# A delta-rule attention and a maxout network: the second group's triangular solve in blocks of 16, kept in SBUF

## The chip, the core and the metric

The kernel runs on one core of a Trainium2 chip. The metric is the device time of one execution in microseconds, as the median of several runs. PE is the matrix engine, DVE the vector engine, ACT the scalar engine, POOL the general-purpose engine; SP only issues transfers.

## The reference

Inputs are q, k, v of 4 batches, 8 heads, 768 steps and 48 dimensions, and a beta per step, all float32. The first layer is a recurrence over the steps; its output, heads side by side, is the input of a maxout network with three weight matrices and an output matrix.

```python
k_n = k / (np.linalg.norm(k, axis=-1, keepdims=True) + 1e-06)
state = np.zeros((B, H, D, D), dtype=np.float32)
for t in range(S):
    kt, vt, bt = (k_n[:, :, t], v[:, :, t], beta[:, :, t, None])
    y[:, :, t] = np.einsum('bhd,bhde->bhe', q[:, :, t], state)
    v_old = np.einsum('bhde,bhd->bhe', state, kt)
    state = state + bt[:, :, :, None] * np.einsum('bhd,bhe->bhde', kt, vt - v_old)
...
x = attn_out.transpose(0, 2, 1, 3).reshape(B * S, H * D)      # 3072 x 384
h = np.maximum(np.maximum(x @ w1, x @ w2), x @ w3)            # 3072 x 768
out = h @ w_out                                               # 3072 x 384
```

## The kernel before

The 768 steps are cut into 12 chunks of 64 steps. Within a chunk the recurrence is a triangular system per batch and head, whose matrix comes from the products of the chunk's keys; its inverse, times beta, is held as `ut`. Two chunks are a group (six groups, `m` = 0 to 5; chunk `c` belongs to group `c // 2`), and the network works on a group's 512 tokens at a time (`ffn(m)`).

**The solve.** `solve(m)` inverts for all chunks of a group the diagonal blocks at once, one block to a partition: 2 chunks x 2 halves x 32 pairs of batch and head are 128 partitions, each with a block of 32x32 (`BL` = 32, `HB` = 16). One step of it is a pair of DVE instructions: a product into `tmp` (L561) and a subtraction from the solution `y` (L565); row by row, 31 pairs. `FINE` says how many groups are solved in finer blocks: with `m < FINE` each block of 32 is cut into two of 16, both in one instruction, which takes 15 pairs. Before, this is only group 0. Group 1 has its solution in PSUM (`y_p`, L524, one of the three buffers of two banks that all transposes, Gram products and joins take in turn through `ps_two`), zeroed by ACT at L525 and copied out to SBUF in two parts (L567 on ACT, L569 on DVE). Its place in SBUF, `y_bl`, lies in `wo_sb`, which is not yet filled with weights. Groups 2 and later have it in SBUF.

`solve` is a generator: each `yield` ends a step, and the loop around it takes so many steps at a time (`some(solving, n)`; `S1` in the table `FIRST` is one step). After the last step the solution goes to DRAM (`y_d`, L586, two transfers) and comes back in another layout into `ut` (L598, four transfers for each chunk), all on SP's queue.

**The joins.** Four products put the blocks together. Where blocks of 16 were solved, `halves_t` (three DVE transposes, L645 and L647), `halves_z` (32 products, L685, and an ACT copy L688) and `halves_u` (32 products, L696, and four ACT multiplications L700 that write into `ut`) make blocks of 32 of them. Then `join_z` (L713), `turn_t1` (L630, L632) and `join_u` (L726) make blocks of 64. `new` (L771) applies `ut` to the values. `halves_z` multiplies whole rows of 64, so the quarter of `ut` that no transfer writes must be zero: `new` clears it after use (L781) where the buffer is used again for a group in fine blocks. There are two buffers of `ut`, for chunks of even and odd number.

**The order around it.** All is ordered by hand: each engine executes its instructions in the order in which the code issues them, and waits at each for what it needs. After a first part (group 0's keys, solve and chunk 0), the loop over `ffn(0)` interleaves the network of group 0 with the rest of the attention. Each of its 31 steps, `i`, begins with one group of products of the network (L1224: three products of 256 columns for `i` < 18, of 512 behind, and from `i` = 27 the output's, L1262; two PSUM buffers), whose result ACT copies (L1232, one in three) or DVE takes the maximum with (L1238). Then come, by tables keyed by `i`: `FIRST` (the links of chunk 1, named by a letter and a number: `e` halves_z, `f` halves_u, `z` join_z, `d` turn_t1, `j` join_u, `k` and `q` products with the state, `u` new, `s` the state's update L801, `y` and `x` the output and its transposes, `T` transposes of queries, followed by a load of later queries on SP; `S` steps of the solve; `M` a mask L399, `P` Gram products of queries), `EARLY_LINKS` (the same letters for chunks 2 and 3, and `t` and `g`, transposes L338 and Gram products L415 of the units of group 2), a conversion of a piece of weights (`conv`: three ACT instructions L247 to L249, one DVE L259, one POOL L263), further steps of the solve, and loads of keys, queries, values and weights. Group 2's solve begins at `i` = 20.

Of the kernel before, what the change touches and what calls it, by code (L numbers as in the profile page):

```python
# [18 lines left out]
BL = 32  # L19
HB = 16  # L20
# [3 lines left out]
def kernel(  # L24
# [31 lines left out]
    nc = tc.nc  # L56
# [9 lines left out]
    GROUPS = UNITS // 4  # L66
    TOK = 512
    NK, NQ, NU = 8, 3, 2
    FINE = 1

    const = ctx.enter_context(tc.tile_pool(name="const", bufs=1))
    work = ctx.enter_context(tc.tile_pool(name="work", bufs=2))
# [19 lines left out]
    def ps_two(name):  # L92
        return pairs.tile([128, 2, 512], FP32, name=name, tag="two", bufs=3)
# [103 lines left out]
    t1 = [const.tile([128, 2, H, BL], FP32, name=f"t1{i}") for i in range(NU)]  # L197
# [254 lines left out]
    def in_rows(t):  # L452
        return t.rearrange("p s r -> p (s r)")[:, 0 : BL * BL].rearrange(
            "p (j i) -> p j i", i=BL
        )


    def in_wo(i):
        n = BL * BL + BL
        return wo_sb.rearrange("p t d -> p (t d)")[:, n * i : n * (i + 1)].rearrange(  # L460
            "p (s r) -> p s r", s=2
        )
# [44 lines left out]
    def solve(m):  # L507


        x = in_rows(xs[m])  # L510
        if m == 1:
            y_bl = in_wo(1)
        else:
            y_bl = work.tile([128, 2, HB * BL + HB], FP32, name="y_bl", bufs=1)
        done = y = in_rows(y_bl)
        zero = kpad[0][:, 0:1, D : D + 1]
        if m in (0, 2):
            nc.gpsimd.memset(y_bl, 0.0)
        elif m > 2:
            nc.scalar.copy(y, zero.to_broadcast(y.shape))  # L520
        bl = small("bl", BL)
        norm(bl, diagonal(x), small("root_bl", BL), small("nt_bl", BL))
        if m == 1:
            y = ps_two("y_p").rearrange("p b (j i) -> p (b j) i", i=BL)  # L524
            nc.scalar.copy(y, zero.to_broadcast(y.shape))  # L525
        if m:
            norms_of(m, bl)
            nc.vector.reciprocal(bl, bl)
        else:
            bl_0.append(bl)  # L530
            bl = small("inv_bl", BL)
            nc.vector.reciprocal(bl, bl_0[0])
        nc.vector.tensor_tensor(out=bl, in0=bl, in1=bl, op=ALU.mult)
        nc.vector.tensor_tensor(out=bl, in0=bl, in1=beta_bl[:, m] if m else beta_0, op=ALU.mult)
        if m > 2:
            nc.scalar.copy(diagonal(y), bl)
        else:
            (nc.vector if m == 1 else nc.gpsimd).tensor_copy(diagonal(y), bl)
        if m < FINE:
            size, xv, yv = HB, in_blocks(xs[m]), in_blocks(y_bl)  # L540
            xb = xv[:, :, :, 0:HB]
            by = bl.rearrange("p (s i) -> p s i", i=HB)[:, :, None, :]
            by = by.to_broadcast([128, 2, HB, HB])
        else:
            size, xv, yv = BL, x[:, None], y[:, None]
            xb, by = x, bl[:, None, :].to_broadcast([128, BL, BL])
        nc.vector.tensor_tensor(out=xb, in0=xb, in1=by, op=ALU.mult)
        yield
        for j in range(size - 1):
            a, b = j + 1, size - 1 - j  # L550
            n = BL // size
            tmp = work.tile([128, 256], FP32, name="tmp", bufs=1)
            t_v = tmp[:, 0 : n * a * b].rearrange("p (s c i) -> p s c i", s=n, i=b)
            row, column, rest = (
                xv[:, :, j, None, j + 1 : size],
                yv[:, :, 0:a, j, None],
                yv[:, :, 0:a, j + 1 : size],
            )
            if n == 1:
                row, column, rest, t_v = (t[:, 0] for t in (row, column, rest, t_v))  # L560
            nc.vector.tensor_tensor(  # L561
                out=t_v, in0=row.to_broadcast(t_v.shape),
                in1=column.to_broadcast(t_v.shape), op=ALU.mult,
            )
            nc.vector.tensor_tensor(out=rest, in0=rest, in1=t_v, op=ALU.subtract)  # L565
            if m == 1 and j == BL - 8:
                nc.scalar.copy(done[:, :, 0:HB], y[:, :, 0:HB])  # L567
            elif m == 1 and j == BL - 2:
                nc.vector.tensor_copy(done[:, :, HB:BL], y[:, :, HB:BL])  # L569
            yield  # L570
        if m == 0:
            back = in_rows(xs[0])
            nc.vector.transpose(out=back, in_=y.rearrange("p c i -> p i c"))
            yield
            for i in range(4):
                if i % 2:
                    n = H * (i == 3)
                    if n:
                        placed(0, i, nc.vector.tensor_copy, slice(0, n))
                    placed(0, i, nc.scalar.copy, slice(n, 2 * H))  # L580
                else:
                    placed(0, i, nc.vector.tensor_copy)
            return
        y_d = dram.tile([2, 2, B, H, BL, BL], FP32, name="y_d")
        for cc in range(2):
            nc.sync.dma_start(  # L586
                out=y_d[cc].rearrange("f b h i j -> (f b h) i j"),
                in_=done[64 * cc : 64 * (cc + 1)],
            )
        yield  # L590
        for cc in range(2):
            for half in range(2):
                for bb in range(2):
                    r0 = C * bb + BL * half
                    (
                        (nc.sync, nc.gpsimd) if m == GROUPS - 1
                        else one_queue if m or cc else both_queues
                    )[bb].dma_start(  # L598
                        out=ut[cc][
                            r0 : r0 + BL, :, :, BL * half : BL * (half + 1)  # L600
                        ].rearrange("p g h i -> p (g h) i"),
                        in_=y_d[cc, half, 2 * bb : 2 * bb + 2].rearrange(
                            "b h c i -> c (b h) i"
                        ),
                    )
            yield
# [158 lines left out]
    def new(c):  # L765
        rhs = rhss.pop(c)
        u = us[c] = both("u", D, 2)
        for hs, p_v, copy in heads_of(c, "p_u", D):
# [7 lines left out]
            copy(u[:, :, span(hs)], p_v)  # L776
        if c + NU < 2 * FINE:
            for bb in range(2):
# [497 lines left out]
    def some(gen, n):  # L1276
        for _ in range(n):
            if next(gen, gen) is gen:
                break

    conv = weights()
    solving = solve(0)
# [71 lines left out]
    for _ in range(2):  # L1354
# [17 lines left out]
    solving = solve(1)  # L1372
# [26 lines left out]
        GROUPS - 2: {0: 2, 1: 3, 2: 3, 3: 3, 4: 3, 5: 3},  # L1399
    }  # L1400
    EARLY_LINKS = {
        9: "k0 q0", 10: "t0", 11: "t1", 12: "g0", 13: "t2", 14: "g1", 15: "t3",
        16: "g2", 17: "g3", 18: "d0 d1 z0 z1", 19: "j0", 20: "j1 u0", 21: "s0",
        23: "k1 y0 q1", 24: "u1 x0", 25: "s1", 26: "y1", 28: "x1",
    }


    FIRST = {
        0: "e1 s0 S1 S1", 1: "f1 k1 S1 S1 S1", 2: "z1 d1 M2 S1 S1",
        3: "j1 S1 q1 M3 S1 S1", 4: "u1 T4", 5: "y1", 6: "s1 T5", 7: "x1 T6",  # L1410
        8: "T7", 14: "P4", 15: "P5", 21: "P6", 22: "P7",
    }

# [38 lines left out]
    for i, _ in enumerate(ffn(0)):  # L1452
        if i < 7:
            fetch(nc.sync if i else nc.gpsimd)
        if i == 0:
            scale(1, nrm_0[:, 1])
        if i == 1:
            load_q(4)
            load_q(5)
        if i == 2:  # L1460
            load_q(6)
        for _ in range(FETCHED.get(i, 0)):
            fetch(nc.gpsimd)
        if i == 25:
            some(conv, 1)
        if i == 21:
            some(solving, 3)
        queries(FIRST.get(i, ""))
        links(1, EARLY_LINKS.get(i, ""))
        if i == 20:  # L1470
            solving = solve(2)
            some(solving, 1)
        if i in CONVERTED:
            some(conv, 1)
        if i == 0:
            fetch(nc.gpsimd)
        if 3 < i < 14:
            some(solving, (3, 2, 2, 2, 3, 3, 3, 3, 2, 2)[i - 4])
        if i in (8, 13):
            prep_values(i // 4)  # L1480
        if i in (4, 8):
            for n in range(2):
                load_k(8 + 2 * (i > 4) + n, (nc.gpsimd, nc.gpsimd))
        if i == 11:
            load_q(11, (nc.gpsimd, nc.gpsimd))
        if i in (3, 9, 10, 21):
            load_v((3, 9, 10, 21).index(i) + 2)
        if i == 18:
            blocks(2)
        if i == 23:  # L1490
            prep_values(4)
        if i > 21:
            some(solving, (3, 1, 2, 2, 3, 5, 5, 5, 5)[i - 22])
        if i in (27, 28, 29):
            load_blocks(i - 15, nc.sync)
        if i in (15, 17, 19, 22, 25, 27):
            less_first((15, 17, 19, 22, 25, 27).index(i))
        if 27 <= i < 30:
            turn_first((2 * (i - 27), 2 * (i - 27) + 1))
# [5 lines left out]
    for m in range(1, GROUPS):  # L1505
        for i, _ in enumerate(ffn(m)):
# [6 lines left out]
            if m + 2 < GROUPS:  # L1513
                if i == 6:
                    blocks(m + 2)
                if i == 8:
                    solving = solve(m + 2)
# [37 lines left out]
```

## Time and profile before

| | us |
|---|---|
| median of 3 runs | 505.97 |
| lowest and highest | 505.88, 508.54 |
| span of the profiled execution | 505.2 |
| PE busy | 484.0 |
| DVE busy | 361.1 |
| POOL busy | 187.1 |
| ACT busy | 169.4 |

Lines named L... are those of the kernel before. A busy time counts an instruction from its start to its end; a matmul's end is modelled. In the stage-by-stage view the number in brackets is a count of instructions; one product of the code is two matmuls in the trace. The DMA share is the mean busy share of the 16 DMA engines. In the waits, a row is a waiting engine and line, what released it, and the total, the number of times and the longest. The chain of waits goes back from the last instruction, at each step to what released it.

Where the second group's solve lies: its 31 pairs begin at 52.4 us and end at 88.5; the loop over `ffn(0)` runs from 44.9 to 158 us; chunk 2's join (L713) begins at 104.9.

### The profile page before, as it was taken

To read this page: it belongs to the slowest core of one execution; us is meant where nothing else is said; L and a number is where in the kernel's file an instruction comes from. 1 tells how busy PE (TensorE), PEld (TensorE's weight loads), DVE (VectorE), ACT (ScalarE), POOL (GpSimd) and SP (SyncE) were. 2 spreads that over 40 slices of the span, in tenths; PEclk is the share of its full clock that TensorE was granted. 3 is DMA by queue.
4 is the path that set the end of the run, shared out by engine and by line. 5 is a ranking of instruction groups with operands and counts; after the bars stand their busy time and mean duration, and the time that the engine had idled before them with its cause. 6 is when DMAs were issued, how large, how long until landed. Compare 5 with 4: busy or idle time off the path is not lost.

```text
span 505.2 us, 18676 instructions
## 1 busy us (share of the span) xinstructions
PE 484.0 (96%) x8064; PEld 338.0 (67%) x8064; DVE 361.1 (71%) x835; ACT 169.4 (34%) x320; POOL 187.1 (37%) x311
## 2 busy tenths in 40 slices
PE   7678989999999999999999999999999999999996
PEld 6467767855566555565565565555797457998895
DVE  5888799787996441799652999565998874468753
ACT  5585664885422142210152200242201032212210
POOL 7434472793391935770395880501000020000000
PEclk9855899999999999999999999999999999999999
DMA  8937869864045934544584652744224230340002
GB/s 114 205 50 214 195 142 160 198 181 137 3 120 134 191 72 77 146 119 117 112 156 104 158 137 74 149 72 96 64 54 90 47 86 15 85 94 1 0 18 47
DMA packets 109121, 53.50 MB, mean 106 GB/s; under 512 B 92208, under 2 KB 102864, under 8 KB 109040
## 3 DMA queue, kind: packets, MB, share of 16 engines
q1 hardware_dynamic: 97280, 31.78, 31.0%
q0 software_dynamic: 9216, 19.85, 16.5%
q8 instruction: 63, 1.03, 0.9%
q10 hardware_dynamic: 2544, 0.69, 0.8%
q14 instruction: 18, 0.15, 0.1%
HBM read 39.17 MB, written 13.11 MB: 103 GB/s over the span
## 4 chain that ended last, share of the span: by engine, by line
PE 76%; DVE 11%; ACT 4%; DMA 3%; SPq 3%; issue 2%; POOL 0%; DVEq 0%; ACTq 0%; POOLq 0%
PE p_h L1224 28%; PE p_o L985 13%; PE p_o L1262 12%; PE p_c L1163 5%; DVE tmp L561 3%; PE p_g L415 2%; PE p_m L905 2%; PE p_u L771 2%; PE p_k L743 2%; DVE y_p L565 2%; DMA kmore<-in_k_dram 2%; PE p_y L813 2%; PE p_s L794 2%; PE p_q L743 1%; PE p_j L726 1%
## 5 line engine op out<-in xcount | busy, mean ns | idle before, releaser
L1224 PE MATMUL p_h<-xt,w_sb 128*128 128x512 f32 (+1 forms) x450 | 186.8, 558 | 0.6 <-ACT xt L839 0.6
L1224 PEld LDWEIGHTS p_h<-xt,w_sb 128*128 128x128 f32 x450 | 82.4, 193 | 69.2 <-issue 61.6
L1238 DVE TENSOR_TENSOR h<-h,p_h 128x512 f32<-128x512 f32 (+1 forms) x42 | 25.5, 607 | 46.8 <-PE p_h L1224 46.3
L565 DVE TENSOR_TENSOR y_bl<-y_bl,tmp 128x31 f32<-128x31 f32 (+20 forms) x139 | 50.4, 363 | 4.8
L561 DVE TENSOR_TENSOR tmp<-x_bl,y_bl 128x31 f32<-128x31 f32 (+20 forms) x139 | 48.8, 351 | 3.9
L1262 PE MATMUL p_o<-wo_sb,h 128*128 128x384 f32 x144 | 48.9, 490 | 0.0
L373 POOL DMA_DIRECT2D turned<-in_q_dram x72 | 39.3, 554 | 4.6 <-POOL turned L368 3.1
L1262 PEld LDWEIGHTS p_o<-wo_sb,h 128*128 128x128 f32 x144 | 26.7, 190 | 17.2
L1234 ACT ACTIVATE h<-p_h 128x512 f32<-128x512 f32 x24 | 14.3, 597 | 69.2 <-PE p_h L1224 69.2
L263 POOL TENSOR_TENSOR w_sb<-mant,up 128x384 int32<-128x384 int32 x18 | 19.0, 1054 | 39.5 <-DVE mant L259 37.8
L415 PEld LDWEIGHTS p_g<-kqt 48*64 48x64 f32 x1216 | 24.5, 142 | 9.2 <-issue 6.3
L415 PE MATMUL p_g<-kqt 48*64 48x64 f32 (+1 forms) x1216 | 27.7, 241 | 0.9 <-ACT kqt L344 0.8
L1268 ACT COPY o_sb<-p_o 128x384 f32<-128x384 f32 x12 | 5.8, 479 | 62.6 <-PE p_o L1262 56.5
L801 DVE TENSOR_TENSOR st<-st,p_s 48x768 f32<-48x768 f32 (+1 forms) x18 | 17.1, 949 | 12.7 <-PE p_s L794 12.4
L399 DVE TENSOR_TENSOR pt<-p_g,mask 128x512 f32<-128x512 f32 x20 | 13.8, 690 | 17.0 <-PE p_g L415 16.9
L598 POOL DMA_DIRECT2D ut<-y_d x4 | 2.6, 653 | 60.6 <-DMA y_d<-y_bl 60.6
L148 POOL DMA_DIRECT2D v_t<-in_v_dram x14 | 11.6, 832 | 35.3 <-PE p_u L771 35.3
L368 POOL MEMSET turned<- 128x96 f32 x18 | 3.3, 191 | 49.4 <-DVE kqt L389 49.4
L771 PEld LDWEIGHTS p_u<-v_t,ut 64*64 64x64 f32 x768 | 13.5, 141 | 8.4 <-issue 7.3
L432 ACT COPY at<-p_g 128x512 f32<-128x512 f32 x22 | 12.8, 585 | 17.4 <-DVE pt L399 15.4
L373 POOL DMA_DIRECT2D turned<-in_k_dram x32 | 17.5, 556 | 1.2 <-POOL turned L368 1.2
L1163 PE MATMUL p_c<-xt,w_sb 128*128 128x256 f32 x72 | 17.7, 379 | 0.0
(239 smaller groups left out, 907.3 us busy)
## 6 DMA issues: line engine op xcount, KB each, us to landing
w_bits<-in_moe_w_dram SPq DMA_DIRECT2D x9, 384.0 KB, 6.2
w_bits<-in_moe_w_dram POOLq DMA_DIRECT2D x9, 384.0 KB, 5.7
turned<-in_q_dram POOLq DMA_DIRECT2D x72, 48.0 KB, 2.8
out_dram<-o_sb SPq DMA_DIRECT2D x36, 96.0 KB, 2.3
y_x<-y SPq DMA_DIRECT2D x32, 96.0 KB, 3.0
qall<-y_x SPq DMA_DIRECT2D x32, 96.0 KB, 2.8
v_t<-in_v_dram POOLq DMA_DIRECT2D x14, 192.0 KB, 5.0
at_d<-at SPq DMA_DIRECT2D x72, 32.0 KB, 3.0
```

The costliest lines, as they stand in the source:

```text
L263: nc.gpsimd.tensor_tensor(out=dst.bitcast(I32), in0=mant_v.bitcast(I32), in1=up_v, op=ALU.add)
L373: (queue, nc.gpsimd)[i].dma_start(out=t[p0 : p0 + 32, bb, at : at + NP * 2 * D].rearrange("p (j x) -> p j x", j=NP), in_=(k, q)[i][2 * bb ...
L415: nc.tensor.matmul(p_g[rows(bb ^ (g * i)), par, c0 : c0 + C * (1 + whole)], kq[:, 0], kq if whole else kq[:, i],)
L561: nc.vector.tensor_tensor(out=t_v, in0=row.to_broadcast(t_v.shape), in1=column.to_broadcast(t_v.shape), op=ALU.mult,)
L565: nc.vector.tensor_tensor(out=rest, in0=rest, in1=t_v, op=ALU.subtract)
L771: nc.tensor.matmul(p_v[rows(bb ^ g), g, i], ut[c % NU][rows(bb), g, h], rhs[rows(bb), g, h],)
L801: nc.vector.tensor_tensor(out=s_v[r], in0=s_v[r], in1=p_s[r, :, 0 : H * D], op=ALU.add)
L985: nc.tensor.matmul(to[:, g], a[j][:, 128 * g : 128 * (g + 1)], b[j], start=(start and g == j == 0), stop=(stop and g == 1 and j == len(a) ...
L1163: nc.tensor.matmul(to, w[stays], moves, start=(n == 0), stop=(n == len(terms) - 1))
L1224: nc.tensor.matmul(p_h, w_sb[i][:, t, f * 128 : (f + 1) * 128], xt[:, t, lo : lo + w], start=(t == 0), stop=(t == KT - 1),)
L1238: nc.vector.tensor_tensor(out=h, in0=h, in1=p_h, op=ALU.max)
L1262: nc.tensor.matmul(p_o, stays, moves, start=(n == 0), stop=(n == len(terms) - 1))
```

## The change

Group 1 is solved in fine blocks too (`FINE` = 2), its solution is in SBUF from the start, the two copies out of PSUM are gone, chunks 2 and 3 get the joins `e` and `f`, and the solve's steps are redistributed.

```diff
-    FINE = 1
+    FINE = 2
...
         if m == 1:
-            y = ps_two("y_p").rearrange("p b (j i) -> p (b j) i", i=BL)
-            nc.scalar.copy(y, zero.to_broadcast(y.shape))
+            nc.scalar.copy(y_bl, zero.to_broadcast(y_bl.shape))
...
             nc.vector.tensor_tensor(out=rest, in0=rest, in1=t_v, op=ALU.subtract)
-            if m == 1 and j == BL - 8:
-                nc.scalar.copy(done[:, :, 0:HB], y[:, :, 0:HB])
-            elif m == 1 and j == BL - 2:
-                nc.vector.tensor_copy(done[:, :, HB:BL], y[:, :, HB:BL])
             yield
...
     EARLY_LINKS = {
-        9: "k0 q0", 10: "t0", 11: "t1", 12: "g0", 13: "t2", 14: "g1", 15: "t3",
-        16: "g2", 17: "g3", 18: "d0 d1 z0 z1", 19: "j0", 20: "j1 u0", 21: "s0",
+        9: "k0 q0", 10: "t0", 11: "t1", 12: "g0 e0", 13: "t2 e1", 14: "g1", 15: "t3 f0",
+        16: "g2 f1", 17: "g3", 18: "d0 d1 z0 z1", 19: "j0", 20: "j1 u0", 21: "s0",
...
     FIRST = {
-        0: "e1 s0 S1 S1", 1: "f1 k1 S1 S1 S1", 2: "z1 d1 M2 S1 S1",
-        3: "j1 S1 q1 M3 S1 S1", 4: "u1 T4", 5: "y1", 6: "s1 T5", 7: "x1 T6",
+        0: "e1 s0 S1", 1: "f1 k1 S1 S1", 2: "z1 d1 M2 S1 S1",
+        3: "j1 S1 q1 M3 S1", 4: "u1 T4", 5: "y1", 6: "s1 T5", 7: "x1 T6",
...
-        if 3 < i < 14:
-            some(solving, (3, 2, 2, 2, 3, 3, 3, 3, 2, 2)[i - 4])
+        if 3 < i < 9:
+            some(solving, (2, 2, 2, 2, 3)[i - 4])
```

By `FINE`, `new(0)` and `new(1)` now also clear the quarter of `ut` (`if c + NU < 2 * FINE`), two ACT copies of 32 partitions each. Lines from L570 on are five lower in the changed kernel. In the built program, PE has four more groups of 32 products, ACT ten more instructions for these joins and four for the clearing, and one less for the copy out; DVE has 15 pairs instead of 31, one copy less and six transposes more. On SP's queue the transfers of `y_d` and into `ut` move ahead of two loads of values and of one set of writes of `at_d`; the other instructions of SP and all of POOL keep their order.

## The prediction, made before the changed kernel was run

> **What bounds the kernel now.** I read the shares and the forty slices first, then the chain of waits of the part that the change touches, then the busy time stage by stage.
>
> ```profile
> PE 484.0 (96%) x8064; PEld 338.0 (67%) x8064; DVE 361.1 (71%) x835; ACT 169.4 (34%) x320; POOL 187.1 (37%) x311
> ...
> PE   7678989999999999999999999999999999999996
> ...
> PEclk9855899999999999999999999999999999999999
> ```
>
> A slice is 12.6 us. PE is full from the eighth slice on (88 us); what idle time it has lies before that. The second solve runs on DVE from 52 to 89 us. The chain of waits from 40 to 132 us (start, length, what) makes it look decisive:
>
> ```profile
> 88.53 0.69 DVE wo_sb L569
> ...
> 92.37 4.47 DMA y_d<-wo_sb
> 97.21 1.47 SPq L598
> ...
> 102.94 2.33 DMA at_d<-at
> ...
> 130.66 1.15 PE p_u L771 x64
> ```
>
> The solve's end, its trip through DRAM and the reads back follow one another, until DVE work releases the matmul of L771 at 130.66. But the busy time by stage (columns: length, then busy us of PE, PEld, DVE, ACT, POOL, then clock, DMA share, GB/s) says what that is worth:
>
> ```profile
> 40.00:55.00 15.00, 13.66 (x306) 11.40 (x306) 10.76 (x29) 7.77 (x17) 8.17 (x9) 0.56 0.82 210
> 55.00:70.00 15.00, 13.37 (x409) 10.88 (x400) 13.41 (x34) 13.29 (x27) 5.64 (x7) 1.00 0.65 152
> 70.00:88.00 18.00, 16.25 (x275) 13.57 (x276) 16.74 (x45) 7.42 (x13) 8.24 (x11) 1.00 1.08 174
> 88.00:102.00 14.00, 14.00 (x302) 11.58 (x294) 10.71 (x20) 12.03 (x25) 10.14 (x13) 1.00 0.83 194
> 102.00:140.00 38.00, 37.85 (x906) 21.82 (x897) 33.75 (x68) 22.41 (x42) 21.79 (x30) 1.00 0.37 104
> ```
>
> From 88 to 140 us PE idles 0.15 us: the chain that ends at L771 is only 0.15 us later than PE's own work. So a shorter solve can win only PE's idle time before 88 us, 1.34 + 1.63 + 1.75 = 4.7 us; and every matmul added behind 88 us is paid in full. Of the 4.7 us, the waits name 1.0 us for a query load and 0.7 for an update of the state; the timeline of PE adds 0.5 us before L726, for DVE transposes (L630, L632), and 1.0 us put down to issue:
>
> ```profile
> PE p_t L338 <- DMA qall<-in_q_dram: 1.0, 1, 1.0
> ...
> PE p_x L832 <- DVE st L801: 0.7, 1, 0.7
> ```
>
> **The change part by part.** *DVE.* L561 and L565 of this solve are 31 pairs, 10.37 + 10.83 = 21.2 us, and L569 takes 0.69. Fifteen pairs on two blocks of 16 stand in the trace for the first group: 17.76 to 26.40 us, 8.6 us. Those operands all lie in SBUF; the third group's 31 pairs, also in SBUF, take 24.3 us where the same 31 with PSUM take 21.2, the excess being operations that stretch to 1.06 us beside a POOL addition. So the new pairs cost 8.6 to 11.7 us. Added are two sets of transposes (L645, L647: 0.71 + 1.44 = 2.15 us each). DVE loses about 7 net. That is off the path behind 88 us; before it, it can close the 0.5 us before L726. The freed PSUM buffer (three instead of two for all the halves and joins) closes the 0.7 before L832. Gain: 1.2 us, between 0 and 3.7 (all idle but the query load).
>
> *ACT ahead of the loop.* `new(0)` now clears two corners of `ut`, 32x512 each: 0.59 us each by L717 on the same shape, 1.04 by the slowest 32x512 copy (L505). They must wait until PE has read `ut`, about 40.2 us, and stand ahead of three weight conversions, the copy of `y` and the zeroing of the solution, for which the transposes into `xt` and then the first L1224 (44.92) wait; PE has nothing else there. Placed one behind the other: corners to 41.4, conversions (1.57) to 43.0, `y` to 43.4, zeroing to 44.6, second `xt` copy 45.0 to 45.5. So 0.6 us later, 0 to 1.6. The same two copies in `new(1)` fall at 67 us, ahead of ACT's idle stretch from 71 (1.3 and 2.4 us waits for PE): nothing; if that cover were gone, 1.2.
>
> *PE.* Two of `halves_z` and two of `halves_u`, each 32 products, shown as 64 matmuls, run behind 88 us. The only such group at full clock is L696:
>
> ```profile
> 53.70 1.14 PE L696 MATMUL p_f<-z,t 64*64 64x32 f32 x64
> 54.65 1.13 PE L743 MATMUL p_k<-st,kqt 48*64 48x48 f32 x64
> ...
> 57.20 0.75 PE L713 MATMUL p_z<-ut,at 32*32 32x32 f32 x64
> ```
>
> Starts 53.77 and 54.83 give 1.06 us (the last digits by the chain's rows). L685 was run only at half clock, 1.86 us; beside it L794 took 1.73 at half and 1.08 at full clock, so L685 would be 1.16. The cheapest row of 64, on 32x32 tiles, takes 0.68. So 4 x 1.06 = 4.2 us, between 2.7 and 4.6.
>
> *ACT behind 88 us.* Two copies of z (0.59) and eight of L700 (0.39) are 4.3 us, among some 13.5 us of old work in the same steps (six conversions of 1.57, two of L344, three of L432, one of L1232). PE needs about 19 us for these steps with the new products. ACT follows in order and fits: nothing, up to 2 if a PSUM buffer is given back late.
>
> *The trip through DRAM, moved.* It goes from i = 12 and 13 to i = 8 on SP's queue: two writes of `y_d`, eight reads into `ut`, now ahead of two loads of v and one set of `at_d` writes, and behind the query loads:
>
> ```profile
> 72.29 8.76 SPq L129 DMA_DIRECT2D qall<-in_q_dram  x6
> 81.14 5.71 SPq L148 DMA_DIRECT2D v_t<-in_v_dram  x4
> ...
> 92.37 1.15 SPq L586 DMA_DIRECT2D y_d<-wo_sb  x2
> 96.85 5.00 SPq L598 DMA_DIRECT2D ut<-y_d  x8
> ```
>
> The solve is done by about 74 us, but the last query load waits for PE's T7 (77 us), and its issue is slow (8.76 us for six, at a DMA share of 1.08): SP is free at about 81. Before, from the first write's issue (92.37) four reads were issued by 100.3 and landed some 2.3 us later: 10.3 us. So `ut` of chunk 2 is there at 91.3, or 93 if the query loads (landing 8.3 us after issue at 78.5) hold the writes up. PE asks for it in the first new product (i = 12, right behind L415, which ended at 88.7): with 1.2 gained and 0.6 lost, and the query load that made it wait until 85.84 coming hardly sooner, at 88.4. PE stands 2.9 us, between 0 and 5. DVE's L645 waits for the same reads, and behind it L1238; it is ready again before PE needs that buffer. Chunk 3's reads are issued 2 us after chunk 2's, PE wants them 3.3 us after: no wait. The loads of v that now come behind are wanted at 97 us by POOL's scaling (4 us behind PE there), and land at about 98: nothing, up to 1 us.
>
> Sum: PE stands 0.4 us earlier at 88.4 (the rest of the 0.6 net waits for the query load), then +2.9 and +4.2: **+6.7 us**. The profiled execution spans 505.2 us and would span 511.9; the median of the runs is 0.77 above that span, so **512.7 us**.
>
> The clock: it fell to half at 25.79 us and stayed there for 27.3 us. In the 3.4 us before, PE was busy 0.87 us:
>
> ```profile
> 22.38:25.79 3.41, 0.87 (x32) 0.70 (x24) 3.02 (x12) 0.81 (x2) 0.00 (x0) 1.00 1.10 199
> 25.79:29.20 3.41, 2.13 (x66) 1.80 (x64) 3.24 (x6) 3.14 (x7) 0.00 (x0) 0.50 0.47 77
> ```
>
> [...] By the rows it is a rival.
>
> **The rivals.** *The reads are in time* (no wait at i = 12): 0.6 - 1.2 + 4.2 = +3.6, 509.6. For it: y_d's landing can be 3.1 us instead of 4.5, and without the loads of v the DMAs are freer after 82. Against it: SP is not free before 80 and eight issues take 5 us.
> *Not slower*: the products are as cheap as L713's (2.7 us), the reads are in time, and the shorter DVE queue and the third buffer close the PE gaps between 40 and 88 us, 3.7 of 4.7: -1.0 us, 505.0. It decides from the point where the gaps closed are worth more than the products. For it: the chain of waits, which runs through this solve. Against it: the waits with a name that DVE or the buffer owns are 1.2 us, and 64x64 tiles have never run at L713's price.
> *The clock falls*: the wait at i = 12 leaves a window mostly idle, and the next 27.3 us run at half clock, where L794 takes 1.73 for 1.08: 27.3 x (1 - 1.08/1.73) = 10.3 us more, 523.0. For it: the two rows above. Against it: windows 2.4 of 3.4 us busy (63.34, 83.82) kept the clock.
>
> **How the numbers follow.** Wait at i = 12: 0.50 (510 to 516.5 alone). In time: 0.25. Clock: 0.10. Not slower: 0.15. The predicted time is that of the likeliest, 512.7. The range 507.0 to 518.0 leaves out most of the clock's case and half of the last. Half a per cent, 2.5 us, is about what this kernel's runs tell from no change: faster by more 0.04 and within 0.12 come from the last case and the cheap edge of the second; slower 0.84.
>
> **What would show it.** Right: L685 at i = 12 idles behind DMA of `ut`; the four new groups take 1.0 to 1.1 us each; the solve ends near 74 us; L832 no longer waits for L801; the first L1224 starts near 45.5; behind i = 17 every stage is shifted by one amount. Wrong: no idle time before L685 at i = 12, or PE reaching i = 12 before 86 us, or idle time in PE between 95 and 140 us that was not there.

## The result, and the profile after

| | kernel before | changed |
|---|---|---|
| median, us (4 runs each, same chip) | 505.93 | 520.17 |
| lowest to highest, us | 505.4 to 508.54 | 518.75 to 524.55 |
| span of the profiled execution, us | 505.2 | 518.3 |

The changed kernel is slower: ratio 1.0269, 95% interval 1.0228 to 1.0311. On another chip (below) it was 1.0198, 1.0132 to 1.0263. The forecast was 512.7 us, range 507 to 518: the direction was right, the size was not. All ratios are estimated from the fast runs of both kernels, without the disturbed slow ones, so they are not the quotients of the medians.

Lines of the changed kernel from L570 on are five lower than those quoted so far (L1224 is now L1219, L685 is L680, L713 is L708), and L561 and L565 are L560 and L564. Its page, in the same two views as above:

```profile
PE 492.2 (95%) x8320; PEld 345.1 (67%) x8320; DVE 351.7 (68%) x808; ACT 175.2 (34%) x333; POOL 186.5 (36%) x311
...
PEclk9756999699999999999999999999999999999999
```

PE has 256 matmuls more, as announced; DVE is 9 us less busy. New is the 6 in the eighth slice of the clock row (91 to 104 us). The timeline of PE there (start, length, line, shape, count, and in brackets the idle time before with its releaser):

```profile
86.53 1.10 PE L415 MATMUL p_g<-kqt 48*64 48x128 f32 x32
90.91 0.42 PE L680 MATMUL p_e<-ut,at 64*64 64x32 f32 x4 [3.27 <-DMA ut<-y_d]
93.25 1.92 PE L680 MATMUL p_e<-ut,at 64*64 64x32 f32 x60 [1.92 <-DMA ut<-y_d]
95.09 2.93 PE L1219 MATMUL p_h<-xt,w_sb 128*128 128x256 f32 x6
97.81 1.06 PE L338 MATMUL p_t<-ident,kpad 128*128 128x128 f32 x4
```

PE came to the first new product at 87.6 us and stood 5.2 us for the reads into `ut`. Behind it everything is slow: six matmuls of L1219 in 2.9 us where 1.5 is usual. The stage views say why (columns as above):

```profile
70.00:88.00 18.00, 17.64 (x312) 15.16 (x304) 9.70 (x22) 10.33 (x19) 8.84 (x11) 1.00 1.01 186
88.00:102.00 14.00, 9.18 (x146) 7.89 (x147) 5.69 (x10) 4.47 (x9) 3.42 (x4) 0.63 0.93 164
...
86.74:90.16 3.42, 0.90 (x32) 0.65 (x24) 0.69 (x1) 1.86 (x5) 1.56 (x3) 1.00 0.81 141
90.16:93.57 3.41, 0.75 (x16) 0.64 (x20) 0.34 (x1) 0.00 (x0) 0.00 (x0) 0.50 0.81 177
93.57:96.98 3.41, 3.41 (x62) 2.99 (x58) 2.14 (x4) 1.77 (x4) 1.00 (x1) 0.50 0.97 164
```

In the 3.4 us up to 90.16 PE was busy 0.90 us; then the granted clock fell to half and stayed there until 100.40, though from 93.57 on PE was wholly busy. And SP's queue shows why the reads were late:

```profile
73.35 6.24 SPq L129 DMA_DIRECT2D qall<-in_q_dram  x6
79.68 1.52 SPq L581 DMA_DIRECT2D y_d<-wo_sb  x2
86.30 6.41 SPq L593 DMA_DIRECT2D ut<-y_d  x8
92.75 3.02 SPq L148 DMA_DIRECT2D v_t<-in_v_dram  x4
```

The solve ended at 77.5 us, but its writes stood behind the query loads until 79.68. They took 6.3 us to land (4.9 for the same writes in the kernel before), and the reads, issued from 86.30 on, 3.0 to 4.0 us (median 3.6; 2.2 to 4.1, median 3.1, for the same eight in the kernel before). The last that PE needed was there at 93.2, 13.5 us behind the first write's issue.

To compare executions whose beginnings differ by some us, I use four marks on PE: the first product of the network (L1224), the Gram products at i = 12 (first L415 of 48x128), the first `join_z` of chunk 2 (L713) and the end. The marks to Gram, from Gram to join, and from join to end were 42.80, 17.20 and 400.28 us before, and 40.86, 30.66 and 401.14 after. The loss lies in the second, +13.46 us; the others give +0.75 (up to the first mark), -1.94 and +0.86, 13.1 us in all. The medians differ by 14.2.

### The profile page after: what moved, and what is told of

The parts are those of the page before. It is cut to its first block, busy times and chain, and to the rows that moved or that the text cites. A ratio compares the mean times of both kernels' runs of the same rounds, so it can differ in the third digit from the quotient of the medians.

```text
span 518.3 us, 19183 instructions
## 1 busy us (share of the span) xinstructions
PE 492.2 (95%) x8320; PEld 345.1 (67%) x8320; DVE 351.7 (68%) x808; ACT 175.2 (34%) x333; POOL 186.5 (36%) x311
## 3 DMA queue, kind: packets, MB, share of 16 engines
q8 instruction: 65, 1.06, 0.9%
## 4 chain that ended last, share of the span: by engine, by line
PE 82%; DMA 6%; DVE 5%; ACT 2%; SPq 2%; issue 2%; POOL 0%; ACTq 0%; POOLq 0%
PE p_h L1219 31%; PE p_o L980 12%; PE p_o L1257 12%; PE p_c L1158 4%; PE p_g L415 3%; PE p_u L766 3%; PE p_y L808 2%; PE p_m L900 2%; PE p_k L738 2%; DMA kmore<-in_k_dram 2%; PE p_s L789 2%; PE p_q L738 2%; PE p_j L721 2%; SPq L129 1%; DMA x_bl<-at_d 1%
## 5 line engine op out<-in xcount | busy, mean ns | idle before, releaser
L1219 PE MATMUL p_h<-xt,w_sb 128*128 128x512 f32 (+1 forms) x450 | 189.2, 563 | 1.1 <-ACT xt L834 0.6
L1219 PEld LDWEIGHTS p_h<-xt,w_sb 128*128 128x128 f32 x450 | 83.2, 195 | 70.3 <-issue 62.4
L560 DVE TENSOR_TENSOR tmp<-x_bl,y_bl 128x31 f32<-128x31 f32 (+20 forms) x139 | 50.7, 365 | 3.9
L564 DVE TENSOR_TENSOR y_bl<-y_bl,tmp 128x31 f32<-128x31 f32 (+20 forms) x139 | 48.5, 349 | 4.8
L415 PEld LDWEIGHTS p_g<-kqt 48*64 48x64 f32 x1216 | 24.8, 143 | 9.4 <-issue 6.5
L415 PE MATMUL p_g<-kqt 48*64 48x64 f32 (+1 forms) x1216 | 28.2, 242 | 0.9 <-ACT kqt L344 0.8
L796 DVE TENSOR_TENSOR st<-st,p_s 48x768 f32<-48x768 f32 (+1 forms) x18 | 17.1, 950 | 12.6 <-PE p_s L789 12.3
L148 POOL DMA_DIRECT2D v_t<-in_v_dram x14 | 11.5, 829 | 36.2 <-PE p_u L766 36.2
L766 PEld LDWEIGHTS p_u<-v_t,ut 64*64 64x64 f32 x768 | 13.5, 143 | 7.9 <-issue 5.9
L750 DVE TENSOR_TENSOR v_t<-v_t,p_k 128x768 f32<-128x768 f32 x11 | 10.4, 950 | 10.8 <-PE p_k L738 4.6
```

Source lines behind the costliest of these rows:

```text
L415: nc.tensor.matmul(p_g[rows(bb ^ (g * i)), par, c0 : c0 + C * (1 + whole)], kq[:, 0], kq if whole else kq[:, i],)
L560: nc.vector.tensor_tensor(out=t_v, in0=row.to_broadcast(t_v.shape), in1=column.to_broadcast(t_v.shape), op=ALU.mult,)
L766: nc.tensor.matmul(p_v[rows(bb ^ g), g, i], ut[c % NU][rows(bb), g, h], rhs[rows(bb), g, h],)
L1219: nc.tensor.matmul(p_h, w_sb[i][:, t, f * 128 : (f + 1) * 128], xt[:, t, lo : lo + w], start=(t == 0), stop=(t == KT - 1),)
```

## The experiments

Each is named by its label; the medians are of one chip in each group, and so is the ratio's interval.

| run | median (before) | ratio, interval | to Gram | Gram to join | join to end |
|---|---|---|---|---|---|
| kernel before, profile | 505.93 | | 42.80 | 17.20 | 400.28 |
| changed kernel, profile | 520.17 (505.93) | 1.0269, 1.0228-1.0311 | 40.86 | 30.66 | 401.14 |
| e1 joins later | 518.0 (508.22) | 1.0156, 1.0083-1.0229 | 43.27 | 23.69 | 401.51 |
| e2 SBUF alone | 511.95 (508.22) | 1.0065, 1.0033-1.0097 | 45.91 | 17.20 | 401.44 |
| e3 busy in the wait | 519.78 (508.22) | 1.0229, 1.0172-1.0286 | 41.03 | 27.65 | 403.24 |
| e4 products alone | 511.99 (508.22) | 1.007, 1.0039-1.01 | 42.25 | 22.15 | 401.01 |
| e5 values later | 510.8 (508.37) | 1.0044, 1.001-1.0079 | 41.15 | 17.19 | 405.12 |
| e6 writes sooner | 517.09 (508.37) | 1.0126, 1.0051-1.0202 | 39.78 | 24.45 | 400.45 |
| e7 without joins | 513.23 (508.37) | 1.0087, 1.0055-1.0119 | 43.89 | 17.20 | 405.10 |
| e8 changed again | 519.06 (508.37) | 1.0198, 1.0132-1.0263 | 40.71 | 29.77 | 400.29 |
| e9 all mended | 517.78 (508.26) | 1.0184, 1.0142-1.0225 | 41.52 | 27.93 | 401.74 |
| e10 one load later | 509.29 (508.26) | 1.0028, 0.9995-1.006 | 42.33 | 17.19 | 403.81 |
| e11 shifted blocks, one run | 518.66 (505.65) | | 46.02 | 22.11 | 402.49 |

**The wait or the products (e1, e4).** e1:

```diff
-        9: "k0 q0", 10: "t0", 11: "t1", 12: "g0 e0", 13: "t2 e1", 14: "g1", 15: "t3 f0",
-        16: "g2 f1", 17: "g3", 18: "d0 d1 z0 z1", 19: "j0", 20: "j1 u0", 21: "s0",
+        9: "k0 q0", 10: "t0", 11: "t1", 12: "g0", 13: "t2", 14: "g1", 15: "t3 e0",
+        16: "g2 e1 f0", 17: "g3 f1", 18: "d0 d1 z0 z1", 19: "j0", 20: "j1 u0", 21: "s0",
```

> The changed kernel with its four new joins three steps and less later: e0 at i = 15, e1 and f0 at 16, f1 at 17 instead of 12, 13, 15, 16. Theory (the time is the wait for the reads into ut at i = 12, 5.2 us, and the half clock that follows from it, 2.6 us): the reads land at 93.2 us, PE comes to e0 at about 95, no idle time before it, the clock stays full behind 70 us, and the run takes 509 to 511 us. Rival A (the products and joins themselves, or ACT behind 88 us, are what costs): still 516 us or more. Rival B (the solve in SBUF or the corners cost on the way to i = 12): still 518 or more.

e4, in the kernel before:

```diff
+    def more(n):
+        p_v = ps_two("p_e")[:, :, 0 : H * BL].rearrange(
+            "p g (h x) -> p g h x", x=BL
+        )
+        for h in range(H):
+            for bb, g in TILES:
+                t = ats[n + g][rows(bb), h]
+                nc.tensor.matmul(p_v[rows(bb ^ g), g, h], t, t[:, 0:BL])
...
         links(1, EARLY_LINKS.get(i, ""))
+        if i in (12, 13, 15, 16):
+            more(4 + 2 * (i % 2))
```

> The kernel before with four more groups of 32 products of 64x64 by 64x32 behind the links of i = 12, 13, 15 and 16; their results are not used. Theory: four times 1.06 us and no wait, 510.2 us, between 509 and 511. Rival A (such products behind 88 us cost much more than their own time, by PSUM buffers or ACT): 513 us or more. If they hide in gaps: 506 to 507.

In e1 the wait for reads is gone, the clock holds there, and the stretch takes 23.69 us, 6.97 less than in the changed kernel. In e4 the bare products lengthen it by 4.95 (this profile is the slowest of e4's ten runs; its median is 3.8 us above the kernel before). So of the 13.46 us about 5 are the products and the rest goes with the joins' early place.

By the median alone e1 speaks for rival A: 518.0 lies not at 509 to 511 but at "516 or more". On this chip the kernel before ran at 508.22, 2.3 us above the 505.93 from which these values were set; less that, e1 would be at 515.7. Of the 11.7 us by which e1's span exceeds that of the kernel before, 6.5 lie in the stretch, 4.81 without an issue gap of 1.68 us in it: that is what the products cost in e4. Another 3.5 lie ahead of the first L1219, which came at 48.40 us, as it came at 48.24 in e4, whose program up to there is that of the kernel before; so that late start isn't the change, and its cause is open. On the way to Gram e1's profile lost 3.0 us at L721, put down to issue (2.2 in the changed kernel), with the clock at half from 65.6 to 72.4 behind it. That gap comes back below.

**The clock (e3).**

```diff
-        links(1, EARLY_LINKS.get(i, ""))
+        if i == 12:
+            links(1, "g0")
+            busy(24, ident)
+            links(1, "e0")
+        else:
+            links(1, EARLY_LINKS.get(i, ""))
```

> The changed kernel with 24 more products of the identity with itself on PE between g0 and e0, some 5.3 us of work that nobody reads, put where PE waits for the reads. Theory (the clock falls because PE idles there): the clock stays at full behind 87 us, e0 still starts at about 93.2, and the time falls by 2 to 3 us, to about 517.5, though PE does more. Rival (the clock falls for another reason, or is no cost): the clock falls all the same and the time is 520 or more.

```profile
87.14 5.62 PE L1288 MATMUL p_w<-ident 128*128 128x128 f32 x48
92.97 1.28 PE L680 MATMUL p_e<-ut,at 64*64 64x32 f32 x64 [0.20 <-DMA ut<-y_d]
```

The timeline of PE in e3: useless work fills the wait, the reads come at the same time as in the changed kernel, the clock never falls behind 53.7 us, and the stretch takes 27.65 instead of 30.66 us. The fall of the clock was worth 3.0 us between these two profiles. The medians (ratios 1.0229 and 1.0198 to 1.0269, on different chips) are too far spread to show it.

**The trip through DRAM (e6), and the changed kernel again (e8).**

```diff
-            some(solving, (2, 2, 2, 2, 3)[i - 4])
+            some(solving, (2, 2, 2, 3, 2)[i - 4])
```

> The changed kernel with the writes of y_d one step of the loop sooner, ahead of the last query load on SP's queue (the solve's steps per i are 2, 2, 2, 3, 2 instead of 2, 2, 2, 2, 3). Theory (the wait at i = 12 is the trip through DRAM, late because the writes stand behind the query loads): the writes are issued at about 77.7 us instead of 79.7, the reads land 2 us sooner, the wait falls from 5.2 to about 3 us. The stage from L415 at i = 12 to L713 of chunk 2 takes 28.5 us if the clock still falls, 26 if it holds (30.7 in the changed kernel). Rival (the reads are late for the DMA load between 80 and 93, whenever they are issued): 30 or more.

> The changed kernel once more, unaltered, on the chip of the other three. 12 to 15 us over the kernel before, the wait of about 5 us before L680 and the fall of the clock behind it, as in its first profile.

The timeline of SP's queue in e6:

```profile
77.36 2.76 SPq L581 DMA_DIRECT2D y_d<-wo_sb  x2
...
83.68 4.76 SPq L593 DMA_DIRECT2D ut<-y_d  x8
```

And of PE, at its first joins:

```profile
88.90 1.39 PE L680 MATMUL p_e<-ut,at 64*64 64x32 f32 x64 [1.43 <-DMA ut<-y_d]
```

The writes left at 77.36, 2.3 us sooner than in the changed kernel's first profile and 3.1 sooner than in e8 (80.49); the wait was 1.43 us, the clock held, and the stretch took 24.45. In e8 the wait was only 2.64 us, but the clock fell twice, for 3.4 us each, once behind it and once behind a gap of 1.56 us at L415 put down to issue: 29.77. The trip through DRAM, begun behind the query loads, is what PE waited for. The run as a whole gained less than the stretch: e6's profile is of the fastest of its four runs, 513.04 us, and the others took 516.9 to 521.9.

**The solution in SBUF (e2).**

```diff
-            y = ps_two("y_p").rearrange("p b (j i) -> p (b j) i", i=BL)
-            nc.scalar.copy(y, zero.to_broadcast(y.shape))
+            nc.scalar.copy(y_bl, zero.to_broadcast(y_bl.shape))
...
-            if m == 1 and j == BL - 8:
-                nc.scalar.copy(done[:, :, 0:HB], y[:, :, 0:HB])
-            elif m == 1 and j == BL - 2:
-                nc.vector.tensor_copy(done[:, :, HB:BL], y[:, :, HB:BL])
```

> The kernel before with one part of the change: the second solve stays in blocks of 32, but with the solution in SBUF and without the copies out of PSUM. Theory: PE no longer waits before L832 for L801 (0.7 us), POOL's additions stretch some DVE pairs without PE noticing; 504.5 to 506.5 us. Rival B (the solution in SBUF is what costs): 510 us or more.

The ratio is 1.0065. The median of 511.95 is above rival B's 510, but with this chip's kernel before 2.3 us above the 505.93 from which the values were set, it comes to 509.7, between the two. The 31 pairs took 12.74 + 13.46 = 26.2 us (21.2 with PSUM). A line of its timeline of DVE:

```profile
75.34 2.19 DVE L560 TENSOR_TENSOR tmp<-wo_sb 128x255 f32<-128x255 f32 x1
```

And one of PE's, some 3 us on:

```profile
78.91 1.12 PE L338 MATMUL p_t<-ident,qall 128*128 128x128 f32 x4 [3.23 <-DVE st L796]
```

An operation of 0.42 us takes 2.19 us (POOL's L296 runs beside it from 75.75 to 77.24; elsewhere in that run 1.1, also beside POOL's work), L796 is late behind it, PE stands 3.23 us for a PSUM buffer, and the clock falls for 3.4 us: 45.91 us to Gram. So in this profile SBUF alone is a loss; in the changed kernel, with 15 pairs (5.46 + 6.14 = 11.6 us), PE has no such wait.

**The shorter solve alone (e7).**

```diff
-        9: "k0 q0", 10: "t0", 11: "t1", 12: "g0 e0", 13: "t2 e1", 14: "g1", 15: "t3 f0",
-        16: "g2 f1", 17: "g3", 18: "d0 d1 z0 z1", 19: "j0", 20: "j1 u0", 21: "s0",
+        9: "k0 q0", 10: "t0", 11: "t1", 12: "g0", 13: "t2", 14: "g1", 15: "t3",
+        16: "g2", 17: "g3", 18: "d0 d1 z0 z1", 19: "j0", 20: "j1 u0", 21: "s0",
```

> The changed kernel without the four new joins of chunks 2 and 3 (e0, e1, f0, f1 left out; group 1's blocks of 32 lack their off-diagonal 16x16 part). Theory: what the shorter solve and the freed PSUM buffer bring by themselves is the idle time of PE ahead of i = 12, and nothing behind: first L1224 to L415 41 us (42.8 before), L415 to L713 17.2 as before, and 1 to 2 us less than before in all. Rival (the chain of waits through the solve sets the end, as the chain view of the kernel before reads): 5 us or more less than before.

The run leaves out the four joins, and with them a part of the inverse. It is 0.9% slower than the kernel before, not faster: the chain-of-waits reading (5 us or more less) is out, and so is my 1 to 2 us less. The stretch from Gram to join is 17.20 us, to the digit. On the way to Gram PE stood 3.58 us at L721 (issue), and the clock was at half for 6.8 us behind that. Behind the join it lost about 5 us, by a wait that I had priced at up to 1. Rows of the waits of e7:

```profile
ACT mant L247 <- POOL w_sb L263: 7.0, 2, 5.1
POOL v_t L296 <- DMA v_t<-in_v_dram: 6.3, 1, 6.3
...
PE p_j L721 <- ACT z L712: 3.0, 2, 2.6
```

The loads of values now stand behind the reads into `ut`; POOL waits 6.3 us for them, ACT's conversions wait for POOL, the copies of z stand behind the conversions, and PE waits 3.0 us; the clock falls again. In the changed kernel, where everything behind PE's own wait at i = 12 is later, POOL came to these values at 102.0 us and found them there.

**The loads of values in the kernel before (e5, e10).**

```diff
-        if i in (3, 9, 10, 21):
-            load_v((3, 9, 10, 21).index(i) + 2)
+        if i in (3, 11, 12, 21):
+            load_v((3, 11, 12, 21).index(i) + 2)
```

> The kernel before with its loads of values for chunks 3 and 4 at i = 11 and 12 instead of 9 and 10; all else as before. In the changed kernel these loads stand behind the reads into ut, and PE's wait of 1.0 us for a query load (L338, 85.84) was gone. Theory: the small packets of these loads held that query load up; without them the wait is gone here too, and the stage from the first L1224 to L415 at i = 12 takes 41.8 us instead of 42.8, the run 1.0 us less. Rival (the query load is late by its own issue): the wait stays, no change.

> The kernel before with only the load of values for chunk 4 later, at i = 14 and so behind the reads into ut on SP's queue; chunk 3's stays where it is. The run with both loads later lost its gain to the reads, which came late. Theory: the query load's wait before L338 (1.0 us) is shortened, the reads are not late, first L1224 to L415 42 us, L415 to L713 17.2; the run 0 to 1 us less than before. If the chunk 3 load alone is what holds the query load up: no change.

e10 has `(3, 9, 14, 21)` in the same two lines. In both the wait for the query load before L338 is gone: the loads of values had held it up. In e5 the time to Gram is 41.15 us as expected, but then PE stands 2.40 us before L713 for the reads, which now come behind these loads, and the clock falls: 1.0044. e10 is inconclusive in time (1.0028, 0.9995 to 1.006); its profile has a wait of 2.37 us before L743 for the state's update at 128 us, which the kernel before doesn't have; that the moved load causes it isn't shown. In both, PE lost more behind the join than it had won before Gram (4.84 against 1.65 us in e5, 3.53 against 0.47 in e10).

**All mended (e9), and the issue gaps (e11).** e9 has e6's order, chunk 3's values ahead of the reads, and e0 and e1 one step later:

```diff
-        9: "k0 q0", 10: "t0", 11: "t1", 12: "g0 e0", 13: "t2 e1", 14: "g1", 15: "t3 f0",
+        9: "k0 q0", 10: "t0", 11: "t1", 12: "g0", 13: "t2 e0", 14: "g1 e1", 15: "t3 f0",
...
         queries(FIRST.get(i, ""))
+        if i == 8:
+            load_v(3)
...
-            some(solving, (2, 2, 2, 2, 3)[i - 4])
+            some(solving, (2, 2, 2, 3, 2)[i - 4])
...
-        if i in (3, 9, 10, 21):
-            load_v((3, 9, 10, 21).index(i) + 2)
+        if i in (3, 10, 21):
+            load_v({3: 2, 10: 4, 21: 5}[i])
```

> The changed kernel with three things moved: the writes of y_d ahead of the last query load (as in the run with the writes sooner), the load of values for chunk 3 ahead of the reads into ut and not behind them, and the joins e0 and e1 one step later (13 and 14), f0 and f1 as they were. Theory: no wait before L680, no fall of the clock behind 80 us, no late values; left are the products, 4.2 to 5 us, against 2 to 3 us of idle time closed ahead of i = 12. First L1224 to L415 at i = 12: 40 us; L415 to L713: 22.2 us; the run 1 to 5 us above the kernel before, so still no gain. Rival (the products cost nothing where nothing waits): at or below the kernel before.

e11 is e9 with this at the head of the step:

```diff
+        if i == 9:
+            p_w = ps_ffn([128, TOK], "p_w")
+            for _ in range(30):
+                nc.tensor.matmul(p_w[0:32, 0:8], ident[0:32, 0:32], ident[0:32, 0:8])
```

> The kernel of the run with all three mended, with 30 tiny products of the identity (60 matmuls, 120 instructions, about 0.6 us) on PE at i = 9, whose result nobody reads. In that run PE stood 3.3 us, put down to issue, 5 matmuls before the end of e1 (L680). Theory (PE waits there for the next 16 KB of its instructions: the gaps lie 126 matmuls apart, and each ends 1.3 to 1.5 us behind the end of an instruction packet of the DMA): the gap moves 60 matmuls earlier in the program, to the last matmuls of the Gram products (L415) ahead of e1, or shrinks there, and the gap before the last 10 matmuls of L721 at about 62 us, which lies ahead of the new work, stays where it is. Rival (e1 waits for data or a buffer): a gap stays 5 matmuls before e1's end.

In e9 the wait for the reads is 0.25 us and no values are late, but the run is still 1.0184: PE stands in the middle of e1, for no releaser that the profile shows, and the clock falls for 6.8 us. Timeline of PE in e9, then in e11:

```profile
94.51 1.03 PE L680 MATMUL p_e<-ut,at 64*64 64x32 f32 x57
98.84 0.43 PE L680 MATMUL p_e<-ut,at 64*64 64x32 f32 x5 [3.30 <-issue]
```

```profile
84.39 0.46 PE L738 MATMUL p_q<-st,kqt 48*64 48x48 f32 x6 [2.50 <-issue]
...
98.21 1.68 PE L415 MATMUL p_g<-kqt 48*64 48x64 f32 x96
100.13 1.25 PE L680 MATMUL p_e<-ut,at 64*64 64x32 f32 x64 [0.24 <-issue]
```

With 60 matmuls inserted before, the gap moved to the end of L415's 96, some 60 matmuls earlier in the program, and shrank to 0.24 us; it is no longer inside e1, as it would be if e1 waited for data. The gap before the last 10 matmuls of L721, ahead of the insertion, stayed (1.95 in e9, 0.94 in e11). A new one of 2.50 us came up at L738, with the clock low around it from 81.31 on, behind the tiny products, which had taken 2.06 us. With the joins undisturbed, the stretch takes 22.11 us: 4.91 above the kernel before, what the joins cost with no wait for data. The single run as a whole was still 13 us above the kernel before, most of it outside this stretch.

## Why the prediction was wrong

*PE is full behind 88 us, so a shorter solve wins nothing there*: right. e7 took the joins away and the stretch stayed at 17.20.

*The products, 4 x 1.06 = 4.2 us, at most 4.6*: nearly right. 4.95 in e4 and 4.91 in e11, with some 0.3 us of issue gaps in each.

*PE's idle time before i = 12*: right in kind. The wait before L832 is gone. My assumption that the query load would still hold PE up was not: the loads of values, which were moved, had delayed it. To Gram the changed kernel is 1.9 us and e8 2.1 us shorter (forecast: 0.4 us earlier, after 0.6 lost ahead of the loop), so PE came to the first new product at 87.6 us and not at 88.4.

*The corners, 0.6 us*: right. PE's idle time before the first transposes of `y` was 0.77 us in all five profiles without them (before, e2, e4, e5, e10) and 1.36 to 1.48 in all eight with them.

*The pairs in SBUF, 8.6 to 11.7 us, hidden*: right, 11.6; the hiding depends on there being 15 and not 31 (e2). *ACT behind 88 us, nothing*: right, PE's matmuls had no wait for ACT between Gram and join.

*"PE stands 2.9 us, between 0 and 5"*: the first step that failed, by size. It was 5.2 us, and 2.6 in e8. The route was as described. The solve ended at 77.5 us and not at 74, which cost nothing, as SP came free later still, at 79.7, 1.3 us sooner than I had it. But from the first write's issue to the last read that PE needed it took 13.5 us (10.7 in e8, 11.5 in e6) where I had taken 10.3 from the place the trip was moved from, and PE was there 0.8 us sooner. Why the trip was slower is open: the DMA share was 0.91 during the writes (92.37 to 97.27 us) and 0.77 during the reads (96.85 to 102.94) in the kernel before, and 0.96 (79.68 to 86.00) and 0.78 (86.30 to 93.20) here. What differs is what stands ahead on the queue, six query loads in place of the small `at_d` writes; no run takes all of these away.

*"The clock falls", a rival at 0.10, 10.3 us*: the second step that failed, by its chance, and by its price too. The sum had nothing for it. The row shown, 0.87 us busy of 3.41, spoke for a fall behind a wait like the one forecast, and a fall came in both profiles of the changed kernel. It stayed low 10.24 us (and twice 3.4 in e8), not 27.3, and cost 3.0 us by e3. The 27.3 us came from a stretch where PE was wholly busy only in the last two of eight windows; behind 88 us it is full as soon as the wait is over. As a sum for the stretch: 22.11 us (e11) + 5.19 (wait) + 3.36 (left for the clock) = 30.66. In e8 the wait was inside the forecast, and the stretch hardly shorter: 22.11 + 2.64 (wait) + 1.56 (issue) leave 3.46 for the clock. So the clock is the step that failed in both profiles, the size of the wait in one. The two belong together: with PE kept busy in the wait the clock held at 1.00 (e3), so a chance for the one was a chance for the other, and I weighed them apart. In the changed kernel's first profile the clock fell with PE busy for 0.90 us of the window and came back only after two wholly busy ones. In e8 it also fell after windows that were partly busy (1.46 and 1.86 us), but came back after one busy window each time.

*The gaps put down to issue* were in no term of the sum. They were there before the change too (1.01 us at 65.65), but in e8 one of 1.56 us lay in the stretch, and in e9 one of 3.30.

*The loads of values, up to 1 us*: right here only because PE itself was late; e7 shows 3 us and a fall of the clock.

*"Not slower"*: out, by e4 and e11. Nor did a version come out that beats the kernel before: with the waits for data taken away the joins still cost 4.9 us, against 2 to 3 won before them (1.9, 2.1 and, in e6, 3.0).

What stays open is the last us of the medians, and with it how far each single profile stands for its runs: the unaltered kernel before ran between 505.4 and 516.5 us over these runs, and the profiles show issue gaps and falls of the clock of different sizes in the same program. How often each falls in an execution without a profile wasn't measured.

## What to carry to other kernels

Where PE is full, a chain of waits through another engine is worth only PE's own idle time behind it (17.20 us from Gram to join in e7, as in the kernel before); read the stage's busy times before the chain. When a transfer is moved, don't take its time from its old place (10.3 us there, 13.5 here): count what it is now ahead of and behind, and ask what a wait for it does to the waiting engine's clock (here 10.24 us at half). Trading one engine's work for small matmuls on a full PE must be paid by idle time that PE shows (4.9 us of matmuls against 2 to 3 here).

## What was not expected of the hardware

*PE stands at even distances in the program.* The gaps put down to issue lie about 126 matmuls apart (in the changed kernel before the last 2 of L1219 at 55.98, the last 10 of L721 at 61.66; in the kernel before ahead of the last 17 of L771 at 65.65). One DMA queue of kind "instruction" (q8) shows 63 packets and 1.03 MB for the kernel before, with 8064 matmuls and as many weight loads, and 65 packets and 1.06 MB for the changed one, with 8320 of each: 16,384 bytes a packet, and in both exactly one packet for 128 matmuls. PE goes on 1.3 to 1.6 us behind a packet's end in each of the gaps compared: 64.38 and 65.65 (before), 60.31 and 61.66 (changed), 61.34 and 62.80 (e7), 100.85 and 102.31 (e8), 97.31 and 98.84 (e9), 82.77 and 84.39 (e11), and also the small gap in e11, 98.71 and 100.13. A group of 64 small matmuls takes 1.06 to 1.15 us at full clock, so two of them, as many matmuls as there are to a packet, pass in little more than 2 us; a gap was 0.2 to 3.6 us long. That PE waits in these gaps for its instructions is my estimate from these distances and times and from e11, where the gap moved as the estimate had it; no profile names a releaser, and that the packets queue behind the data was not tried.

*Most falls of the clock came at a wait.* Behind 58 us the clock fell thirteen times in these profiles, for 3.4 to 10.2 us. Twelve of these falls came during a gap of PE of 1.6 to 3.6 us (5.2 in the changed kernel) or within 1.8 us behind its end; the thirteenth, in e11 at 81.31, behind 60 tiny products. But gaps of 1.68 us (e1, at 108 us) and 2.37 us (e10, at 128) brought none, so a gap's length alone did not decide it here. The stage view tells more when it is cut at the clock's own changes, which in each profile lie whole multiples of 3.41 us apart. Two windows of e8, and one of e1 (columns as above):

```profile
89.23:92.64 3.41, 1.46 (x65) 1.34 (x65) 1.20 (x3) 0.58 (x1) 0.50 (x1) 1.00 0.97 201
92.64:96.05 3.41, 3.41 (x11) 2.77 (x12) 1.86 (x5) 2.04 (x4) 1.70 (x2) 0.50 0.94 163
...
106.58:109.99 3.41, 1.82 (x32) 1.59 (x32) 3.38 (x6) 2.18 (x6) 0.67 (x2) 1.00 0.53 139
```

The twelve falls each follow a window in which PE was busy for 0.24 to 1.86 us. The window of e1 above, with 1.82, kept the clock, and so did those with 1.95 us (e3, 63.93) and with 2.04 and 2.42 (e10, the gap of 2.37 us being split between two windows). Ahead of 58 us the clock fell behind 2.14 us too (kernel before, 18.96). So in these profiles the falls sort better by PE's busy time in one such window than by the length of the gap, but not without exceptions, and what sets them is not shown. The thirteenth fall stands apart: its window is wholly busy by the records, over half of it with the tiny products.
